# One pipeline for both spatial-gating halves, and block products for all of the output projection

## The chip, the cores and the metric

The kernel runs on one core of a Trainium2 chip. The metric is the time of one execution on the device, in microseconds (us); a kernel's time is the median of several runs. The core has five instruction streams that run side by side and wait for one another through semaphores: TensorE (PE in the profile; PEld are its weight loads), VectorE (DVE), ScalarE (ACT), GpSimd (POOL) and SyncE (SP, which here only issues DMAs). Each stream executes in the order in which it was written.

## The reference

```python
x = A_x                                            # 1 x 2048 x 1024, bfloat16
h = x + _A_ref(_layernorm(x), wq, wk, wv, wo, beta)    # attention with a memory, 32 heads
h2 = h + _B_ref(_layernorm(h), w_in, w_sp, b_sp, w_out)

def _B_ref(x, w_in, w_sp, b_sp, w_out):
    z = _gelu(jnp.einsum('bsd,df->bsf', x, w_in))      # 2048 x 3584
    z1 = z[..., :1792]
    z2 = _layernorm(z[..., 1792:])
    g = jnp.einsum('ts,bsf->btf', w_sp, z2) + b_sp[None, :, None]
    return jnp.einsum('bsf,fd->bsd', z1 * g, w_out)
```

The change lies in the last two lines: the gate g (w_sp is 2048 x 2048), its product with z1, and the output projection with w_out (1792 x 1024), which is added to h.

## The kernel before

Every instruction goes through a recorder (class `_Recorder`, line 34), which keeps one list for each engine in the order of the calls, works out what each instruction depends on, and puts in the waits. So the order of the calls in the text is the order on each engine's queue, and all instructions have line 210 in the profile; one tells them apart by tile names.

The second half of the program, from 412 us on, has these stages.

**z1 (412 to 491 us).** The gating input z1 is computed transposed, in 14 groups of seven products (`z1_step`, line 1199; the order of the steps is that of `offs`). `on(g, k, ...)` hangs other work behind a step: the layer norm of z2, and, later on, the loads, scalings and sums for the first gate. Each group takes PSUM banks from `next_bank()`.

**The gate for output rows 0 to 1023 (`gate(0)`, line 1087; 491 to 575 us).** A block product of 2 x 2 blocks is done with seven products in place of eight. The blocks of w_sp, transposed and scaled to float16, are b11, b12, b22 and b21, and t1 = b12 - b11, t2 = b22 - t1, t3 = b22 - b12, t4 = b21 - t2 are their sums (`sp_sum`, four quarters each). The blocks of z2 have sums too, `s_sum(1..4, g)`, held in the one buffer SS. There are seven column groups g of 128, and each group ("block" in what follows) has seven products of eight matmuls of 512 columns (`prod`):

- p1 (b11) and p2 (b21) add up in bank g % 3. ScalarE copies the bank after p1 (`copy1`), GpSimd adds a bias to that copy twice (`s1b2`, `s1b1`), and after p2 VectorE finishes the bank (`c11`: an eviction and a multiply `out` by z1).
- t2, t3 and t4 add up in bank bb. VectorE reads it after each of them (u2, u3, and an eviction `VB`).
- t1 and b22 add up in bank bc; VectorE reads it after each (`VB`), each time with an `out`.

TensorE's order in a block g is t2, t1, p1(g+2), t3, p2(g+1), t4, b22; for the last groups p1 is left out or moved. VectorE's order is u2, ss4, ss1 and ss2 of the next group, then whatever `each(g, 0)` and `each(g, 1)` hang there, u3, VB, out, ss3, c11, VB, out, VB, out. A product that adds into a bank waits until the bank's reader is done.

**Output for rows 0 to 1023 (`units`, line 1268, and the loop at 1332; 575 to 624 us).** 16 units, each 14 matmuls of 512 columns in bfloat16 (`out_unit`), then one VectorE add and a store. Between the units stand the preparation of the second gate (its 16 transposed loads of w_sp, `sp_half`, `sp_sum`), the loads and squares of w_out (`wo_norm`), and two scale computations (`scale_y`, `scale_w`): ScalarE's squares are summed over partitions by one small product (`total`), reduced by VectorE, raised to a power by GpSimd, and rounded and spread by VectorE (`power`).

**The gate for rows 1024 to 2047 (`gate(1)`, 624 to 708 us).** The same code. `each1` (line 1411) hangs the scaling of w_out's blocks on ScalarE and their sums (`ob_sum`) on VectorE behind its blocks.

**Output for rows 1024 to 2047 (from line 1462; 708 us to the end).** The same seven-product scheme with seven matmuls a product, in four blocks: `o_p1`, `o_p2`, `o_c11`, the sums `y_sum` of the gated rows on VectorE, three adds on GpSimd (`o_adds`). Six matmuls of the first t2 stand between `o_p1(0)` and `o_p2(0)`.

Of the kernel before, what the change touches and what calls it, by code (L numbers as in the profile page):

```python
# [12 lines left out]
T = 2048  # L13
# [3 lines left out]
L = 512  # L17
# [241 lines left out]
def bass_sequential_preLN__memory_aug_infini_attn__mixer_gmlp__prompt_kernel(  # L259
# [31 lines left out]
    class Bump:  # L291
# [4 lines left out]
        def __call__(self, name, shape, dt):  # L296
# [72 lines left out]
    BH = {k: tens(k + "h", [128, 8, L], F16, o * K)  # L369
          for k, o in ROLES + (("t1", 118), ("t2", 190), ("t3", 22), ("t4", 38))}  # L370
# [22 lines left out]
    TW, YS, INVY, SCW, INVO = [b3(k, [128, 1], F32) for k in ("tw", "ys", "invy", "scw", "invo")]  # L393
    SQY = tens("sqy", [128, 28], F32, 768)
    BSQ = tens("bsq", [128, 2], F32, 896)
    TMP = {k: tens("tmp_" + k, [128, L], F32, (4 + 2 * i) * K)
           for i, k in enumerate(("s1", "s1b1", "s1b2", "u2", "u3"))}
    VB = tens("vb", [128, L], BF16, 61 * K)
    SJ = [tens("sj%d" % i, [128, T], BF16, (4 + 4 * i) * K) for i in range(2)]
    BROW = [tens("brow%d" % i, [128, L], BF16, (205 + i) * K) for i in range(2)]  # L400
    WO0 = [tens("w_out0%d" % i, [128, 7, 512], BF16, o * K) for i, o in enumerate((54, 198))]
    WO1 = [tens("w_out1%d" % i, [128, 7, 512], BF16, o * K) for i, o in enumerate((30, 4))]
    WO0H = [tens("w_out0h%d" % i, [128, 7, 512], F16, o * K) for i, o in enumerate((54, 198))]
    FIN2 = tens("fin2", [128, 4, 2, 2, 512], BF16, 14 * K)
    OT4 = [[tens("ot%d%d" % (i, k), [128, 512], F32, (o + 2 * k) * K) for k in range(4)] for i, o in enumerate((38, 118))]
    SY = [tens("sy%d" % i, [128, 4, 7, 128], F16, o * K) for i, o in enumerate((190, 126))]
    FIN = [tens("fin%d" % i, [128, 512], BF16, o * K) for i, o in enumerate((37, 11, 12, 13))]
# [532 lines left out]
    def scale_of(k, n, b):  # L940
        b = next_bank() if b is None else b
        pe.matmul(PS[:, b, 0:n], ONES[:], SQB[:, 0:n], start=True, stop=True)
        dve.tensor_reduce(out=TOT[:], in_=PS[:, b, 0:n], axis=mybir.AxisListType.X, op=ALU.add)
        dve.tensor_single_scalar(TOT[:], TOT[:], 1e-30, ALU.max)
        if k:
            dve.reciprocal(TOP[:], TOT[:])
        else:
            pool.tensor_tensor(TOP[:], TOT[:], MHZ[:], ALU.pow)
# [48 lines left out]
    for r in range(16):  # L997
        q = (37 * r + 15) // 16
        at(q, sp_norm, r)
        if r < 14:  # L1000
            at(q, sp_norm_load, r + 2)
    at(37, pool.tensor_copy, SQB[:, 0:16], SQ[:])
    for k in range(12):
        at(k + 1, wz_norm, (1, 2, 0)[k // 4], k % 4)
# [44 lines left out]
    def sp_load(pr, k, j):  # L1049
        r0, c0 = 1024 * pr + (512 if k in ("b12", "b22") else 0), 1024 if k in ("b21", "b22") else 0  # L1050
        sp.dma_start_transpose(RAW[k][:, :, j * 128:(j + 1) * 128],
                               B_w_sp[r0 + j * 128:r0 + (j + 1) * 128, c0:c0 + 1024])

    def sp_half(k):
        dve.tensor_single_scalar(BH[k][:], RAW[k][:], SC[0][:], ALU.mult)

    def sp_part(k, r):
        s = slice(2 * r, 2 * r + 2)
        act.activation(BH[k][:, s, :], RAW[k][:, s, :], ACTF.Copy, scale=SC[0][:])
# [3 lines left out]
    def sp_sum(o, r=None, eng=dve):  # L1063
        a, b = SUMS[o]
        s = slice(0, 8) if r is None else slice(2 * r, 2 * r + 2)
        eng.tensor_tensor(BH[o][:, s, :], BH[a][:, s, :], BH[b][:, s, :], ALU.subtract)
# [5 lines left out]
    def s_sum(k, g):  # L1072
        if k == 1:
            dve.tensor_tensor(SS[:, 0], a_blk(1, 0, g), a_blk(1, 1, g), ALU.add)
        elif k == 2:
            dve.tensor_tensor(SS[:, 1], SS[:, 0], a_blk(0, 0, g), ALU.subtract)
        elif k == 3:
            dve.tensor_tensor(SS[:, 2], a_blk(0, 0, g), a_blk(1, 0, g), ALU.subtract)
        else:
            dve.tensor_tensor(SS[:, 3], a_blk(0, 1, g), SS[:, 1], ALU.subtract)  # L1080

    def prod(b, a, w, first):
        for i in range(8):
            pe.matmul(bank(b), a[:, i, :], BH[w][:, i, :], start=(first and i == 0), stop=(i == 7),
                      skip_group_check=True)

    def gate(pr, seam=lambda: None, mid=lambda: None, each=lambda g, k: None):
        inv, zo = (INV[0], Z1T) if pr == 0 else (INVY, Z1X)
        t1, t2 = slice(1024 * pr, 1024 * pr + 512), slice(1024 * pr + 512, 1024 * pr + 1024)
        s1, s1b1, s1b2, u2, u3 = (TMP[k][:] for k in ("s1", "s1b1", "s1b2", "u2", "u3"))  # L1090

        def stt(o, b, add):
            dve.scalar_tensor_tensor(o, bank(b), inv[:], add, ALU.mult, ALU.add)

        def out(v, g, i, t):
            dve.tensor_tensor(zo[:, g + 7 * i, t], v, Z1T[:, g + 7 * i, t], ALU.mult)

        def ss(k, g):
            if g < 7:
                s_sum(k, g)  # L1100

        def p1(g):
            prod(g % 3, a_blk(0, 0, g), "b11", True)

        def copy1(g):
            act.activation(s1, bank(g % 3), ACTF.Copy, scale=inv[:])

        def p2(g):
            prod(g % 3, a_blk(0, 1, g), "b21", False)

        def c11(g):
            stt(VB[:], g % 3, BROW[0][:])
            out(VB[:], g, 0, t1)
# [6 lines left out]
        if not pr:  # L1120
            p1(2)
# [3 lines left out]
        for g in range(7):  # L1125
            bb, bc = 3 + g % 2, 5 + g % 2
            prod(bb, SS[:, 1], "t2", True)
            prod(bc, SS[:, 0], "t1", True)
            stt(u2, bb, s1b2)
            if g == 0:  # L1130
                mid()
            ss(4, g)
            if g:
                ss(1, g + 1)
                ss(2, g + 1)
            if 1 - pr <= g <= 3:
                p1(g + 2)
            each(g, 0)
            prod(bb, SS[:, 2], "t3", False)
            if g < 5:  # L1140
                copy1(g + 1)
                p2(g + 1)
            elif g == 5:
                p1(6)
                copy1(6)
            else:
                p2(6)
            each(g, 1)
            stt(u3, bb, s1b2)
            stt(VB[:], bc, u3)  # L1150
            out(VB[:], g, 1, t2)
            if not g:
                ss(1, 1)
                ss(2, 1)
            if g < 6:
                pool.tensor_tensor(s1b2, s1, BROW[1][:], ALU.add)
            ss(3, g + 1)
            if g != 5:
                c11(min(g + 1, 6))
            prod(bb, a_blk(1, 1, g), "t4", False)  # L1160
            each(g, 2)
            stt(VB[:], bb, s1b1)
            out(VB[:], g, 1, t1)
            if g < 6:
                pool.tensor_tensor(s1b1, s1, BROW[0][:], ALU.add)
            prod(bc, SS[:, 3], "b22", False)
            stt(VB[:], bc, u2)
            out(VB[:], g, 0, t2)
            each(g, 3)

    fins = {}

    def fin_load(u, q=sp):
        tc, lo, w = u
        k = len(fins) % 4
        fins[u] = FIN[k]
        q.dma_start(FIN[k][:, 0:w], out2d[tc * 128:(tc + 1) * 128, lo:lo + w])

    def out_unit(u, wsl, q=sp):
        tc, lo, w = u  # L1180
        b = next_bank()
        mm8(PS[:, b, 0:w], lambda i: Z1T[:, i, tc * 128:(tc + 1) * 128], wsl, n=14)
        fin = fins[u]
        dve.tensor_tensor(fin[:, 0:w], fin[:, 0:w], PS[:, b, 0:w], ALU.add)
        q.dma_start(out2d[tc * 128:(tc + 1) * 128, lo:lo + w], fin[:, 0:w])
# [8 lines left out]
    def z1_out(fc, t, src):  # L1194
        act.activation(Z1T[:, fc, t * 512:(t + 1) * 512], src, ACTF.Gelu_apprx_tanh, scale=INV[1][:])
# [54 lines left out]
    for k, g, r in (("b11", 6, 3), ("b12", 6, 3), ("b22", 8, 3), ("b21", 12, 3)):  # L1250
        for j in range(4):
            on(g, r, sp_load, 0, k, j)
    for n, (k, g) in enumerate((("b11", 8), ("b12", 9), ("b22", 11))):
        for r in range(4):
            on(g, (6, 7, 2, 4)[r], sp_part, k, r)
    for r in range(4):
        on(*((10, 6), (10, 5), (11, 6), (11, 5))[r], sp_sum, "t1", r)
        on(*((12, 5), (12, 6), (13, 3), (13, 6))[r], sp_sum, "t3", r)
        on(*((13, 5), (13, 7), (13, 2), (13, 4))[r], sp_sum, "t2", r)
    on(7, 3, brow_load, 0)  # L1260

    offs = {1: -5, 6: 0, 5: 1, 7: 3, 2: 4, 4: 6, 3: 12}
    for x, g, k in sorted((7 * g + offs[k], g, k) for g in range(14) for k in offs):
        z1_step(g, k)
    for i in range(2):
        sp.dma_start(WO0[i][:], wout[:, 7 * i:7 * i + 7, 0:512])

    units = [(tc, 0, 512) for tc in range(6)] + [(tc, 512, 512) for tc in range(8)] + [(tc, 0, 512) for tc in (6, 7)]
    def seam():
        sp_half("b21")  # L1270
        for k in range(1, 4):
            s_sum(k, 0)

    def mid():
        for r in range(4):
            sp_sum("t4", r)

    def z1_norm(g, k):
        for h in range(k and 2):
            r, o = 2 * g + (k > 2), 1024 + 512 * h  # L1280
            if k != 2:
# [252 lines left out]
```

## Time and profile before

| | us |
|---|---|
| median of 3 runs (755.75 to 756.73) | 756.14 |
| span of the profiled execution, first to last instruction | 753.7 |

The page has no time of its own for the profiled execution beside its span; span and median lie 2.44 us apart. By stage, the engines are busy as follows (us, from the table of stretches of time):

| stretch | length | TensorE | VectorE | ScalarE | GpSimd |
|---|---|---|---|---|---|
| z1, 412.06 to 490.76 | 78.7 | 78.7 | 64.0 | 64.6 | 64.3 |
| first gate, 490.76 to 579.00 | 88.2 | 88.2 | 69.9 | 26.3 | 18.9 |
| first output, 579.00 to 623.76 | 44.8 | 44.8 | 25.8 | 17.1 | 1.9 |
| second gate, 623.76 to 708.47 | 84.7 | 84.7 | 69.7 | 18.2 | 18.1 |
| second output, 708.47 to 754.00 | 45.5 | 42.5 | 30.8 | 2.8 | 16.8 |

The granted clock of TensorE is 1.00 in every stretch. In a line of a timeline the columns are the start, the duration, the engine, the operation, the tile written and the tiles read, their shapes and how many instructions were merged; brackets at the end give how long the engine had been idle and who released it. A matmul's duration includes its way through the array (0.38 us), so one reads the pitch from the starts.

### The profile page before, as it was taken

Reading aid. Unit: us, or ns where it says so; the run is one execution under the profiler, and the core shown is the slowest. Engines: PE = TensorE matmul, PEld = TensorE weight load, DVE = VectorE, ACT = ScalarE, POOL = GpSimd, SP = SyncE. Lnnn points to the kernel's source line nnn. Section 1 sums busy time; section 2 is a strip of 40 time slices with the busy share of each in tenths; the row PEclk is TensorE's granted clock in tenths of the full one; section 3 lists DMA queues with packets and bytes.
Section 4 is the critical chain, followed back from the end, with each engine's and each line's share of the span. In section 5 each row is a group of like instructions: output and inputs, shape, how many; then the busy total and the mean of one; then the engine's idle time right before and its main releaser. Section 6 shows DMA issues by size and latency. Waiting matters only on the chain.

```text
span 753.7 us, 13510 instructions
## 1 busy us (share of the span) xinstructions
PE 748.3 (99%) x5470; PEld 359.1 (48%) x5470; DVE 557.1 (74%) x1013; ACT 421.6 (56%) x519; POOL 296.3 (39%) x450
## 2 busy tenths in 40 slices
PE   9999999999999999999999999999999999999998
PEld 4445455555554445545554444444444444444444
DVE  5585589768975576677986796997885385989776
ACT  6777877787777767325894879733231355300000
POOL 2565456555654334010039988622220011222342
PEclk9999999999999999999999999999999999999999
DMA  9554546444523331678650027330019961001211
GB/s 304 171 164 83 96 75 134 99 72 93 120 58 84 119 79 43 162 188 254 192 169 0 1 41 142 56 98 1 0 21 142 262 198 35 0 1 41 79 50 57
DMA packets 136783, 75.09 MB, mean 100 GB/s; under 512 B 98064, under 2 KB 126480, under 8 KB 136720
## 3 DMA queue, kind: packets, MB, share of 16 engines
q1 hardware_dynamic: 129184, 67.14, 37.0%
q10 hardware_dynamic: 7536, 7.08, 3.5%
q8 instruction: 43, 0.70, 0.4%
q14 instruction: 20, 0.16, 0.1%
HBM read 42.74 MB, written 8.39 MB: 68 GB/s over the span
## 4 chain that ended last, share of the span: by engine, by line
PE 90%; DMA 3%; ACT 3%; DVE 2%; POOL 2%; issue 0%; ACTq 0%; DVEq 0%
PE ps L210 90%; DMA sj<-in_B_w_sp_dram 2%; ACT sj L210 2%; POOL zrs L210 1%; DMA wv<-in_A_wv_dram 1%; POOL sz L210 1%; DVE zst L210 1%; ACT z L210 1%; DVE wzh L210 1%; DVE ht L210 0%; DVE zmv L210 0%; ACT L210 0%; DVE fin L210 0%; ACTq L210 0%; DVE top L210 0%
## 5 line engine op out<-in xcount | busy, mean ns | idle before, releaser
L210 ACT ACTIVATE e<-ps 128x2048 bf16<-128x2048 f32 (+1 forms) x96 | 152.6, 1590 | 41.7 <-PE ps L210 41.5
L210 POOL TENSOR_SCALAR_AFFINE_SELECT e<-e 128x512 bf16<-128x512 bf16 x128 | 90.9, 723 | 131.2 <-ACT e L210 131.2
L210 PE MATMUL ps<-win,hnT 128*128 128x448 bf16 x512 | 98.4, 352 | 0.0
L210 POOL TENSOR_TENSOR tmp_s1b<-tmp_s,brow 128x512 f32<-128x512 f32 x28 | 36.4, 1301 | 121.6 <-DVE tmp_u L210 63.0
L210 PEld LDWEIGHTS ps<-win,hnT 128*128 128x128 bf16 x512 | 49.6, 98 | 46.3 <-issue 0.2
L210 PE MATMUL ps<-xnT,wk 128*128 128x512 bf16 x256 | 60.8, 380 | 0.0
L210 DVE TENSOR_TENSOR zt<-ps,zt 128x512 f32<-128x512 f32 x70 | 48.2, 689 | 16.8 <-PE ps L210 13.5
L210 PE MATMUL ps<-xnT,wq 128*128 128x512 bf16 x256 | 60.5, 379 | 0.0
L210 PE MATMUL ps<-wv,xnT 128*128 128x512 bf16 x256 | 60.0, 381 | 0.3 <-DMA wv<-in_A_wv_dram 0.2
L210 PE MATMUL ps<-wo,oT 128*128 128x512 bf16 x256 | 58.0, 379 | 0.0
L210 ACT ACTIVATE z<-ps 128x448 bf16<-128x448 f32 x60 | 30.4, 545 | 33.4 <-PE ps L210 33.4
L210 PE MATMUL ps<-w_out,z1T 128*128 128x512 bf16 x224 | 48.6, 379 | 0.0
L210 DVE BATCH_NORM_STATS2 zst<-z 128x6 f32<-128x448 bf16 x64 | 37.9, 611 | 10.3 <-ACT z L210 10.2
L210 PEld LDWEIGHTS ps<-v,e 128*128 128x128 bf16 x1280 | 38.8, 96 | 14.0 <-issue 6.5
L210 DVE RECIPROCAL rd<-ps 128x16 f32<-128x16 f32 x32 | 8.0, 250 | 47.0 <-PE ps L210 46.8
L210 PE MATMUL ps<-v,e 128*128 128x33 bf16 x1280 | 42.2, 178 | 0.0
L210 ACT ACTIVATE tmp_s<-ps,invy 128x512 f32<-128x512 f32 x7 | 4.8, 688 | 63.3 <-POOL tmp_s1b L210 35.9
L210 POOL TENSOR_TENSOR sz<-wzh 128x512 f16<-128x512 f16 x28 | 34.5, 1232 | 8.3 <-PE ps L210 8.3
L210 PEld LDWEIGHTS ps<-wo,oT 128*128 128x128 bf16 x256 | 24.1, 98 | 27.5
L210 PEld LDWEIGHTS ps<-xnT,wk 128*128 128x128 bf16 x256 | 22.6, 98 | 29.9 <-issue 5.0
L210 ACT ACTIVATE z1T<-zt,inv 128x512 bf16<-128x512 f32 x42 | 29.0, 715 | 13.1 <-DVE zt L210 13.1
L210 PEld LDWEIGHTS ps<-wv,xnT 128*128 128x128 bf16 x256 | 23.1, 98 | 27.3 <-DMA wv<-in_A_wv_dram 0.9
(204 smaller groups left out, 1459.8 us busy)
## 6 DMA issues: line engine op xcount, KB each, us to landing
sj<-in_B_w_sp_dram SPq DMA_DIRECT2D x16, 512.0 KB, 3.7
xch<-in_A_x_dram SPq DMA_DIRECT2D x16, 256.0 KB, 3.7
xr<-in_A_x_dram SPq DMA_DIRECT2D x16, 256.0 KB, 4.0
out_dram<-hch SPq DMA_DIRECT2D x16, 256.0 KB, 2.4
win<-in_B_w_in_dram SPq DMA_DIRECT2D x4, 896.0 KB, 5.3
wz<-in_B_w_in_dram SPq DMA_DIRECT2D x6, 512.0 KB, 8.0
wo<-in_A_wo_dram SPq DMA_DIRECT2D x1, 2048.0 KB, 8.4
fin<-out_dram ACTq DMA_DIRECT2D x16, 128.0 KB, 3.1
```

Source lines behind the costliest of these rows:

```text
L210: ins = getattr(e, op.name)(*op.args, **op.kw)
```

## The change

- `gate` is replaced by `gates_run`, which runs 14 blocks n without a break: n // 7 is the half of the rows, n % 7 the column group. p1(n+2) and p2(n+1) now cross from the first half into the second. In block 6 there is no p2; block 7 has p2(7), c11(7), p1(9) and p2(8). In block 12 p1(13) takes the place of p2. In blocks 6 and 7 the sums ss1, ss2 and ss3 of the next group go to GpSimd.
- The blocks of w_sp for the second half have their own places in SBUF where they can be loaded while the first half runs: b11 and b12 in block 0, b22 in block 5 after its p1, b21 in block 5 after p2. Scaling on ScalarE in blocks 1 to 4 and 6; the 16 quarter sums on VectorE in blocks 6 and 7.
- Both halves of the gated product are kept scaled in float16. So the first half has a scale too, from a bound that is taken from z1's running sums (`accum_out` in `z1_out`, 28 more accumulator reads) and computed in the z1 stage (`bound_z1`, `scale_y(0, ...)`). `scale_y(1, ...)` stands in block 5 between p2 and u3; b_sp is loaded a second time, squared and added to the bound in the stage before z1.
- The blocks of w_out are loaded in blocks 7 and 8 (two loads, and two times seven), squared on ScalarE in blocks 8 to 10 (28 pieces), `scale_w` stands at the end of block 10, scaling in blocks 11 and 12, and the sums in blocks 11 to 13, with t3's two on GpSimd.
- The 16 units of the first output, and their loads and stores on ScalarE's queue, are gone. The output is eight blocks s of the seven-product scheme. The six matmuls of t2 between `o_p1(0)` and `o_p2(0)` are gone, and three first `y_sum` stand in block 13.
- Some tiles move (VB and the biases into the low area, w_out to 22 K and 46 K, and others).

```diff
-    def gate(pr, seam=lambda: None, mid=lambda: None, each=lambda g, k: None):
+    def gates_run(seam, mid, hook):
...
+        for n in range(NG):
+            pr = n // 7
+            bb, bc = 3 + n % 2, 5 + n % 2
+            se = pool if n in (6, 7) else dve
+            prod(pr, bb, SS[:, 1], "t2", True)
+            prod(pr, bc, SS[:, 0], "t1", True)
+            stt(n, u2, bb, s1b2)
+            if n == 0:
                 mid()
+            ss(4, n)
+            if n:
+                ss(1, n + 1, se)
+                ss(2, n + 1, se)
+            if n == 7:
+                p2(7)
+                c11(7)
+            if 1 <= n < 11:
+                p1(n + 2)
+            hook(n, 0)
+            prod(pr, bb, SS[:, 2], "t3", False)
+            if n == 12:
+                p1(13)
+            if n < 13:
+                copy1(n + 1)
+            if n not in (6, 12):
+                p2(min(n + 1, 13))
+            hook(n, 1)
+            stt(n, u3, bb, s1b2)
+            stt(n, VB[:], bc, u3)
+            out(VB[:], n, 1, 1)
...
+            ss(3, n + 1, se)
+            if n not in (6, 12):
+                c11(min(n + 1, 13))
+            prod(pr, bb, a_blk(1, 1, n % 7), "t4", False)
+            hook(n, 2)
+            stt(n, VB[:], bb, s1b1)
+            out(VB[:], n, 1, 0)
...
+            prod(pr, bc, SS[:, 3], "b22", False)
+            stt(n, VB[:], bc, u2)
+            out(VB[:], n, 0, 1)
+            hook(n, 3)
...
     def z1_out(fc, t, src):
-        act.activation(Z1T[:, fc, t * 512:(t + 1) * 512], src, ACTF.Gelu_apprx_tanh, scale=INV[1][:])
+        acc = {"accum_out": SQY[:, 2 * fc + t:2 * fc + t + 1]} if t < 2 else {}
+        act.activation(Z1T[:, fc, t * 512:(t + 1) * 512], src, ACTF.Gelu_apprx_tanh, scale=INV[1][:], **acc)
...
+    def scale_y(pr, n, b):
+        total(n, b)
+        pool.tensor_tensor(TOT[:], TOT[:], TW[:], ALU.mult)
+        power(YS[pr])
+        dve.tensor_tensor(INVY[pr][:], INV[0][:], YS[pr][:], ALU.mult)
...
+    def bound_z1():
+        dve.tensor_reduce(out=TOP[:], in_=SQY[:], axis=mybir.AxisListType.X, op=ALU.max)
+        dve.tensor_single_scalar(TOP[:], TOP[:], 0.341 * 512, ALU.add)
+        dve.tensor_tensor(TOP[:], TOP[:], TOP[:], ALU.mult)
+        dve.tensor_copy(SQB[:, 0:1], TOP[:])
...
+    on(9, 2, bound_z1)
+    on(9, 4, lambda: scale_y(0, 1, next_bank()))
...
+    on(12, 7, brow_scale, 0)
...
+    for j in range(28):
+        do(j // 6, (0, 0, 1, 2, 2, 3)[j % 6], z1_norm, j)
+    do(5, 0, lambda: pool.tensor_copy(SQB[:], SQY[:]))
+    do(5, 1, scale_y, 1, 28, 7)
+    do(5, 3, brow_load, 1, act)
+    do(6, 0, brow_scale, 1)
+    for k, at_ in (("b11", (0, 0)), ("b12", (0, 0)), ("b22", (5, 0)), ("b21", (5, 2))):
         for j in range(4):
+            do(*at_, sp_load, 1, k, j)
+    for r in range(4):
+        do(1 + r // 2, (0, 2)[r % 2], sp_part, 1, "b11", r)
+        do(3 + r // 2, (0, 2)[r % 2], sp_part, 1, "b12", r)
+        do(6, (0, 0, 1, 1)[r], sp_part, 1, "b22", r)
+        do(6, (3, 3, 3, 3)[r], sp_part, 1, "b21", r)
+    for r in range(4):
+        do(6, (0, 0, 1, 1)[r], sp_sum, 1, "t1", r)
+        do(6, 2, sp_sum, 1, "t2", r)
+        do(6 + r // 2, (3, 0)[r // 2], sp_sum, 1, "t3", r)
+        do(7, (0, 0, 1, 1)[r], sp_sum, 1, "t4", r)
...
     def scale_w():
-        total(8)
+        total(28, 7)
         power(SCW)
-        dve.tensor_tensor(INVO[:], YS[:], SCW[:], ALU.mult)
-        dve.reciprocal(INVO[:], INVO[:])
+        for pr in range(2):
+            dve.tensor_tensor(INVO[pr][:], YS[pr][:], SCW[:], ALU.mult)
+            dve.reciprocal(INVO[pr][:], INVO[pr][:])
-
-    for n, u in enumerate(units):
...
+    do(7, 0, ob_load, "b11")
+    do(7, 0, ob_load, "b21")
+    do(7, 3, ob_load, "b12")
+    do(8, 3, ob_load, "b22")
...
+    do(10, 2, lambda: pool.tensor_copy(SQB[:], SQY[:]))
+    do(10, 3, scale_w)
+    for n, (k, h) in enumerate([(k, h) for k in ("b11", "b12", "b22", "b21") for h in range(2)]):
+        do(11 + n // 4, n % 4, ob_scale, k, h)
+    do(11, 3, ob_sum, "t1", 0)
+    do(12, 0, ob_sum, "t1", 1)
+    do(12, 1, ob_sum, "t2", 0)
+    do(12, 2, ob_sum, "t2", 1)
+    do(12, 2, ob_sum, "t3", 0, pool)
+    do(12, 3, ob_sum, "t3", 1, pool)
+    do(13, 0, ob_sum, "t4", 0)
+    do(13, 1, ob_sum, "t4", 1)
+    do(13, 0, fin_in, 0)
+    do(13, 0, fin_in, 1)
+    for x in range(1, 4):
+        do(13, 2, y_sum, x, 0)
+
+    gates_run(seam, mid, hook)
...
     o_p1(0)
-    for x in range(1, 4):
-        y_sum(x, 0, 6, 7)
     o_adds(0)
-    o_prod(3, o_s(2, 0), "t2", True, cs=range(6))
     o_p2(0)
     o_c11(0)
-    for g in range(4):
+    for s in range(8):
...
+        if s < 4:
+            fin_in(s + 4)
```

`hook(n, k)` calls what `do(n, k, ...)` hung at that place, in the order of the `do` calls. The first piece of an `ob_sum` is 2048 columns wide, the second 1536; `y_sum` has the seven chunks of 128 columns of a block at once.

## Prediction

> **What bounds it now.** I read the page's busy shares first, then the end of the chain of waits, then the timeline of single engines in the stages that the change touches, then the groups of instructions by shape.
>
> ```profile
> PE 748.3 (99%) x5470; PEld 359.1 (48%) x5470; DVE 557.1 (74%) x1013; ACT 421.6 (56%) x519; POOL 296.3 (39%) x450
> ```
>
> ```profile
> 412.06 338.53 PE ps L210 x1578
> ```
>
> From 412.06 us to the end TensorE is one unbroken piece of the chain: every product taken away there is gained, every wait put in there is lost, and nothing later gives it back. The pitch of a 512-column product is the distance between starts: eight take 1.727 us in the gates, so 0.2159 us each. What TensorE needs is released by VectorE, and a steady block (12.09 us, seven groups of eight) shows how:
>
> ```profile
> 537.38 1.89 PE L210 MATMUL ps<-t3h,ss 128*128 128x512 f16 x8
> 539.11 1.89 PE L210 MATMUL ps<-b21h,z2h 128*128 128x512 f16 x8
> 540.83 1.89 PE L210 MATMUL ps<-t4h,z2h 128*128 128x512 f16 x8
> ...
> 539.31 0.75 DVE L210 SCALAR_TENSOR_TENSOR tmp_u<-ps,inv,tmp_s1b 128x512 f32<-128x512 f32 x1 [2.04 <-PE ps L210]
> ```
>
> t3 and t4 add into one bank, and between them VectorE must read that bank (u3). It can start 1.93 after t3 starts and takes 0.75 (0.8 until TensorE moves). Before, the b21 group (p2) lies between and covers this. VectorE's own work is some 9.2 us in 12.09. It is longer where GpSimd works too:
>
> ```profile
> 432.21 1.44 POOL L210 TENSOR_TENSOR sz<-wzh 128x512 f16<-128x512 f16 x1 [0.88 <-PE ps L210]
> 433.73 1.49 POOL L210 TENSOR_TENSOR sz<-sz,wzh 128x512 f16<-128x512 f16 x1
> ...
> 432.55 1.64 DVE L210 TENSOR_TENSOR ht<-hnT 128x1024 f16<-128x1024 bf16 x1
> ```
>
> VectorE's sum (0.68 alone) lasts until GpSimd's first has ended at 433.65 and about half a microsecond more; GpSimd's second (1.16 alone) ends later by as much as it was held. So two-input SBUF instructions of the two take turns, whole instruction by whole instruction. Reads of PSUM (0.75) are not held.
>
> **The change part by part.** Times inside a block count from the start of its first group.
>
> 1. *Products saved.* 16 units of 14 (224) become 4 blocks of 49 (196): 28 x 0.2159 = **-6.05**.
>
> 2. *Before the gates.* One more small copy on GpSimd (0.2) stands in its queue where TensorE already waits 1.0 for it at 412: **+0.2** (0 to 0.2). In the gating-input stage the scale for the first half puts eight small VectorE instructions (0.2 each) and two on GpSimd between them; VectorE falls some 1.9 behind at 469, wins back about 0.43 per group in three groups, and then runs without a gap to 497.4, when it releases the first t2 at 497.67. About 0.6 is left, 0.15 of it spare: **+0.5** (0 to 1.0). The 28 accumulator reads (0.19) add 0.75 per group to ScalarE, which idles 1.2 to 1.4 there; without that cover VectorE's sums would be late by the rest.
>
> 3. *Block 5: the second half's scale.* It stands on VectorE ahead of u3, its small product behind p2.
>
> ```profile
> 608.07 0.15 DVE L210 TENSOR_SCALAR tot<-tot 128x1 f32<-128x1 f32 x1
> ...
> 609.51 0.19 POOL L210 TENSOR_TENSOR tot<-tot,tw 128x1 f32<-128x1 f32 x1
> 609.78 0.57 POOL L210 TENSOR_TENSOR top<-tot,mhz 128x1 f32<-128x1 f32 x1
> 610.38 0.15 DVE L210 TENSOR_SCALAR top<-top 128x1 int32<-128x1 int32 x1 [2.16 <-POOL top L210]
> 610.57 0.15 DVE L210 TENSOR_SCALAR ys<-top 128x1 f32<-128x1 f32 x1
> 610.76 0.16 DVE L210 TENSOR_TENSOR invy<-inv,ys 128x1 f32<-128x1 f32 x1
> ```
>
> p2 ends at 8.64; the reduction starts at 8.86, the maximum at 9.06, GpSimd 9.30 to 10.13, three VectorE steps to 10.7, u3 10.70, t4 at 11.5 instead of 8.64: **+2.9** (2.6 to 3.3). Queued behind it are VB, out, ss3 and c11, so VectorE enters block 6 busy until 2.4.
>
> 4. *Blocks 6 and 7: the swap.* Twelve of the sixteen sums for the second half sit in VectorE's order ahead of an u3 or ahead of the t2 and t3 that read them; six s-sums of 1024 columns move to GpSimd. The trace has no such GpSimd sum; its nearest rows bound it:
>
> ```profile
> L210 POOL TENSOR_TENSOR sz<-wzh,sz 128x512 f16<-128x512 f16 x14 | 16.2, 1156 | 0.0
> L210 POOL TENSOR_TENSOR sy<-z1x 128x128 f16<-128x128 f16 x2 | 0.9, 428 | 11.8 <-DVE z1x L210 11.8
> L210 DVE TENSOR_TENSOR t2h<-b22h,t1h 128x1024 f16<-128x1024 f16 x4 | 2.6, 680 | 0.0
> ```
>
> 128 columns 0.43, 512 columns 1.16, so 1.9 ns a column: 1024 take 2.1, 1536 3.1, 2048 4.1. How long one holds VectorE: at least about 1.1 (the longest hold seen), at most its whole length; I take the whole, since every hold seen lasted to the end. Block 6: u2 2.4, ss4 3.1, then from 3.65 four t1 sums (0.6) and GpSimd's two s-sums (2.1) by turns: 10.2. u3 then, t4 at 11.0 instead of 6.91 (p2 no longer covers: 1.0 of this is there in any case): 4.1. Then VB, out and GpSimd's add to 12.45, four t2 sums and ss3 by turns to 16.9; t2 of block 7, due at 14.45, ends at 17.4 instead of 16.2: 1.2. Two evictions, two outs, add, two t3 sums and ss1 to 22.9, u2 to 23.6: t3, due at 22.6, starts 1.05 late. ss4, GpSimd's ss2 (24.2 to 26.3), c11, two t4 sums, the last two t3 sums to 29.0: t3 ends at 29.5 instead of 25.4, 4.1. Together **+10.5**. With no holding at all the same walk gives 1.0 + 0.1 + 0.15 + 1.5 = 2.75; with holds of 1.1, 5.5; with GpSimd at 2.3 a piece and late loads, 12.5.
>
>    The Trainium skill, page "SBUF — State Buffer", section "Who interferes with whom", says that a VectorE instruction with two SBUF inputs and a GpSimd one that reads SBUF exclude each other for the whole instruction, whichever came first; by that these two blocks cost the 10.5, by the longest hold that the rows show, 5.5.
>
> 5. *Block 10 to 11: the scale of w_out.* After out (1.55) the chain of point 3 with four more small steps ends at 3.6, u2 4.4; t3 has no p1 ahead of it here and was due at 3.5: **+0.9** (0.5 to 1.0).
>
> 6. *Blocks 12 and 13: sums of w_out.* Block 12: t1's and t2's pieces (0.87, 1.15) push u3 to 7.3, t4 to 8.1 instead of 7.0: 1.1. Then GpSimd's t3 pieces (4.1, 3.1) hold ss3 and an out: u2 of block 13 only at 17.6 on block 12's clock, t3 at 18.35 instead of 15.05; ss4 behind the second piece, two t4 pieces, u3 23.25, t4 24.05 where an undisturbed pair of blocks has it at 17.27. Together **+6.8**; with no holding 1.2, with holds of 1.1 about 2; up to 7.5.
>
> 7. *Start of the output.* Six t2 products stood between o_p1(0) and o_p2(0) while ScalarE copied the bank (0.69). Now o_p2(0) follows at once: 1.71 + 0.69 + 0.05 - 1.51 = **+0.95** (0.9 to 1.0).
>
> Costed at nothing: the eight output blocks run as four did, TensorE 49 x 0.2159 = 10.6 against VectorE's 6 x 0.75 + 3.8. SP's queue gets the 16 transposes (1.3 each) in blocks 0 and 5, up to 14 us before use; 16 loads of w_out in 7 and 8, read a block later; and eight output loads, each behind the stores of its buffer (1.7) and some 30 us early. ScalarE's norms and scalings fill 7.2 of 12.1 in blocks 1 to 4, 11.2 in block 8. Its bias loads wait for GpSimd's add at 2.15 of block 6, with eight scalings and the copy for block 7 behind them; landing 3.9, b21 is ready at 16.3, needed at 19.1. With the 8.3 us landing that the same load took on this queue, that is gone and 1 to 2 are lost, inside the bound of 12.5.
>
> Sum: -6.05 + 0.2 + 0.5 + 2.9 + 10.5 + 0.9 + 6.8 + 0.95 = **+16.7**. The profiled span 753.7 becomes 770.4; span and median lie 2.44 apart (756.14), so **772.8 us**.
>
> **Rivals.**
> - *B: holds are short.* GpSimd's long sums hold VectorE only for about 1.1 each. For it: no longer hold is shown. Against: none ended early. Points 4 and 6 become 5.5 and 2: +6.9, **763.0**; with no holds, 2.75 and 1.2, +3.3, 759.5.
> - *C, not slower: VectorE keeps up.* In blocks 6, 7, 12 and 13 its own work (24.1 against TensorE's 24.2 in 6 and 7) runs without any hold and every sum is ready when read. Then only the fixed chains are left: 0.2 + 2.9 + 1.0 (u3 of block 6) + 0.9 + 0.95 = 5.95 against 6.05: **756.0**. It decides from the point where all waits stay under 6.05; for a clear gain they must stay under 4.5, so half of block 5's chain must go too. Against it: the sums' place in VectorE's queue, ahead of u3.
> - *D: more is late* than I walked (bias loads, the seam at 497): above 777.
>
> **How the numbers follow.** The forecast has 0.62, B 0.23, C 0.12, D 0.03. The lows of all terms give -6.05 + 0 + 0 + 2.6 + 2.75 + 0.5 + 1.2 + 0.9 = +1.9, 758; the highs +20.5, 777. That range leaves out C, D and a sliver of B, some 0.17. A measurement of this kernel can tell about 0.2% (1.5 us) from no change: C gives 0.05 to faster and 0.07 to the same, all else, 0.88, is slower.
>
> **What would show it.** Right: TensorE idle of 3 us before block 5's t4, 4 before block 6's t4, 4 inside block 7's t3, 3 each before t3 and t4 of block 13, released by VectorE; GpSimd sums of 1024 columns at 2.1 or more; VectorE's t1, t2, t3 sums well over 0.68 on average; 392 output products. Wrong: TensorE unbroken through blocks 6 and 7, GpSimd's 2048-column piece near 2 us, or VectorE's sums at 0.68 beside it.

## The result, and the profile after

| | before | after |
|---|---|---|
| median of 5 runs each, one chip, us | 755.82 (754.87 to 756.73) | 774.49 (769.87 to 775.92) |
| ratio to before, 95% interval | | 1.0241 (1.0214 to 1.0268) |
| span of the profiled execution, us | 753.7 | 768.1 |

The changed kernel is slower by 18.7 us; 772.8 was forecast. The profiled execution of the changed kernel is the shortest of its five (769.87 us).

The page's line of busy time after, and the view of TensorE's waits from 400 us on (total, number and longest, in us), first before, then after:

```profile
PE 747.5 (97%) x5443; PEld 356.5 (46%) x5443; DVE 583.8 (76%) x1041; ACT 449.1 (58%) x607; POOL 334.2 (44%) x468
```

```profile
PE ps L210 <- POOL sz L210: 1.0, 1, 1.0
```

```profile
PE ps L210 <- DVE tmp_u L210: 11.0, 6, 3.4
PE ps L210 <- DVE t3h L210: 2.5, 1, 2.5
PE ps L210 <- DVE zt L210: 1.1, 1, 1.1
PE ps L210 <- ACT ot L210: 0.8, 1, 0.8
PE ps L210 <- POOL sz L210: 0.2, 1, 0.2
```

TensorE has 27 instructions fewer (28 products less, one small total more), and from 400 us on, where it waited once before (1.02 at 412) and was one unbroken piece of the chain from there, it now waits ten times. tmp_u is u2 or u3: the read of a bank by VectorE between two products that add into it. So most of the time is lost because VectorE is late with a read, not because a sum is missing; only t3h is a sum that TensorE waits for itself. The chain of waits (start, length, what) shows in block 6 what VectorE did in that time:

```profile
571.57 0.76 DVE vb L210
572.35 0.43 DVE z1x L210
572.81 0.76 DVE vb L210
573.63 0.36 issue
574.00 0.74 DVE tmp_u L210
574.73 0.60 DVE ss L210
575.33 6.25 DVE t1h L210 x4
581.59 0.67 DVE tmp_u L210
582.31 11.70 PE ps L210 x40
```

Four sums t1h stand in the chain with 6.25 us, and behind them u3 (tmp_u), which ends as TensorE goes on. Such a sum takes 0.68 alone. The timelines of VectorE and GpSimd in the same block, and in block 12, show why it took longer here:

```profile
575.26 6.33 DVE L210 TENSOR_TENSOR t1h<-b12h,b11h 128x1024 f16<-128x1024 f16 x4
...
662.17 4.55 DVE L210 TENSOR_TENSOR ss<-z2h 128x1024 f16<-128x1024 f16 x1
```

```profile
575.51 2.40 POOL L210 TENSOR_TENSOR ss<-z2h 128x1024 f16<-128x1024 f16 x1 [1.73 <-PE ps L210]
577.99 2.45 POOL L210 TENSOR_TENSOR ss<-ss,z2h 128x1024 f16<-128x1024 f16 x1
...
661.92 4.25 POOL L210 TENSOR_TENSOR z2h<-z2h 128x2048 f16<-128x2048 f16 x1
```

Two GpSimd sums lie inside VectorE's four; in block 12 one VectorE sum of 0.68 lasts 4.55, from just behind the start of GpSimd's long one to about half a microsecond behind its end. The hold lasts the whole instruction.

The losses by place, in the profiled execution, are the shifts of the products' starts against the unbroken pitch:

| place | forecast | measured |
|---|---|---|
| products saved | -6.05 | -6.05 (27 instructions fewer = 28 - 1) |
| up to the first gate product | +0.7 | +0.54 |
| block 5, second scale before u3 | +2.9 | +2.80 |
| blocks 6 and 7 | +10.5 | +9.33 |
| block 10 to 11, scale of w_out | +0.9 | +0.72 |
| blocks 12 and 13 | +6.8 | +6.24 |
| start of the output | +0.95 | +0.94 |
| sum against the span | +16.7 | +14.5 (span: +14.4) |

In the four runs that were not profiled the spans are 772.2 to 773.9, at a mean granted clock of 0.989 to 0.991 instead of 0.993; they have no profile, so this table is of the shortest execution alone. The table of stretches (start:end, length, busy time of TensorE, its weight loads, VectorE, ScalarE and GpSimd, then the granted clock, the DMA share and GB/s) has these rows for the end of block 6, for block 7 and for block 13:

```profile
582.31:588.65 6.34, 6.34 (x16) 2.30 (x17) 6.31 (x7) 4.67 (x5) 3.42 (x2) 0.54 0.07 23
588.65:605.33 16.68, 14.16 (x66) 6.08 (x64) 15.24 (x22) 3.46 (x9) 9.68 (x5) 1.00 0.43 112
670.00:676.20 6.20, 4.99 (x16) 1.80 (x16) 6.17 (x7) 0.00 (x0) 2.94 (x1) 0.72 0.11 20
```

After its wait of 3.42 us TensorE ran t4 and most of b22 at half clock, 6.34 us for 16 products that take 3.45 at full clock; after that of 2.92 us in block 13, t3 took 3.10 instead of 1.73. No clock loss was in the forecast.

### The profile page after: what moved, and what is told of

Same layout as the page of the kernel before. It is cut to its first block, busy times and chain, and to the rows that moved or that the text cites. A ratio compares the mean times of both kernels' runs of the same rounds, so it can differ in the third digit from the quotient of the medians.

```text
span 768.1 us, 13613 instructions
## 1 busy us (share of the span) xinstructions
PE 747.5 (97%) x5443; PEld 356.5 (46%) x5443; DVE 583.8 (76%) x1041; ACT 449.1 (58%) x607; POOL 334.2 (44%) x468
## 4 chain that ended last, share of the span: by engine, by line
PE 80%; DVE 9%; DMA 3%; ACT 3%; POOL 2%; issue 1%; SPq 0%; ACTq 0%; DVEq 0%
PE ps L210 80%; ACT sj L210 2%; DMA sj<-in_B_w_sp_dram 2%; DVE vb L210 2%; POOL zrs L210 1%; DVE ss L210 1%; DVE tmp_u L210 1%; DMA wv<-in_A_wv_dram 1%; POOL sz L210 1%; DVE zst L210 1%; DVE t1h L210 1%; DVE z2h L210 1%; DVE z1x L210 1%; ACT z L210 1%; DVE wzh L210 1%
## 5 line engine op out<-in xcount | busy, mean ns | idle before, releaser
L210 POOL TENSOR_TENSOR ot<-ot,fin 128x512 f32<-128x512 f32 x24 | 32.1, 1363 | 51.6 <-ACT ot L210 51.6
L210 ACT ACTIVATE ot<-ps,invo 128x512 f32<-128x512 f32 x8 | 5.5, 688 | 81.7 <-PE ps L210 81.7
L210 PE MATMUL ps<-z2h,sy 128*128 128x512 f16 (+2 forms) x238 | 49.9, 366 | 0.0
L210 ACT ACTIVATE tmp_s<-ps,invy 128x512 f32<-128x512 f32 x14 | 9.6, 683 | 61.7 <-POOL tmp_s1b L210 55.6
```

The lines of the kernel that those rows point to most:

```text
L210: ins = getattr(e, op.name)(*op.args, **op.kw)
```

## The experiments

Each kernel's ratio is to the kernel before, run on the same chip beside it (median there 756.09, 755.72 and 755.42 in the three sets). What an edit wins is the difference of the medians. The profiled executions of the first three single edits have spans of 767.7, 768.4 and 768.4, no shorter than the 768.1 of the changed kernel, whose profiled execution is the shortest of its five; the section on the three edits together compares them place by place.

### The s-sums of blocks 6 and 7 on VectorE

```diff
-            se = pool if n in (6, 7) else dve
+            se = dve
```

> The six s-sums of blocks 6 and 7 stay on VectorE; nothing else differs from the changed kernel (774.5 us). Theory (GpSimd's sums hold VectorE's): VectorE gets 6 x 0.6 = 3.6 us more work, but no sum is held any more. By the same walk, u3 of block 6 starts at 7.5 on the block's clock in place of 9.7, t4 waits 1.3 in place of 3.6, t3 of block 7 still 2.9, and blocks 6 and 7 together take 28.4 in place of 33.5: about 5 us less and less slow clock, 767 to 770 us. Rival (VectorE simply has too much work there, holds don't matter): 3.6 us more work, 2 to 4 us slower, 776 to 779. Second rival (the slow clock after the wait is the main cost): gain only if the wait falls under the one that triggers it, then about 2 to 4 us.

Measured: 769.56 us (766.76 to 770.27), ratio 1.0173 (1.0152 to 1.0193). VectorE has six sums more and is 4.9 us faster with them. Its timeline in block 6:

```profile
578.86 0.69 DVE L210 TENSOR_TENSOR ss<-z2h 128x1024 f16<-128x1024 f16 x1 [0.38 <-PE ps L210]
579.59 0.69 DVE L210 TENSOR_TENSOR ss<-ss,z2h 128x1024 f16<-128x1024 f16 x1
580.20 2.49 DVE L210 TENSOR_TENSOR t1h<-b12h,b11h 128x1024 f16<-128x1024 f16 x4
```

The two s-sums and the four t1 sums take 3.9 us one behind the other; with the first two on GpSimd the four alone took 6.33. TensorE's wait before block 6's t4 falls from 3.42 to 1.13, the one in block 7's t3 from 2.52 to 2.27. No GpSimd sum lies beside VectorE's t1, t2, t3 and t4 sums any more, so what is left there is the sums themselves in this order, not the holds. In this execution half clock followed block 5's wait of 2.63 (t4 took 3.22 instead of 1.73), which it did not in the changed kernel's.

### The second scale one step earlier

The product, the reduction and GpSimd's power go ahead of p2 of block 5 instead of behind it.

```diff
-    do(5, 1, scale_y, 1, 28, 7)
+    do(5, 0, scale_y, 1, 28, 7)
```

> Only the place of the second half's scale in block 5 moves: behind p1(7), before t3, so that VectorE and GpSimd compute it in VectorE's idle time before u3. Theory (the chain in front of u3 costs 2.8, nothing else): TensorE's wait before t4 of block 5 falls from 2.6 to under 0.3, VectorE enters block 6 some 0.6 earlier relative to TensorE: 3 us less, 771 us. Rival (VectorE's lateness only moves into block 6, where the sums decide): within 1 us of 774.5.

Measured: 770.45 us (769.27 to 771.29), ratio 1.0191 (1.0174 to 1.0208). Block 5 has no wait any more. Block 6's t4 still waits 3.18 and block 7's t3 3.90, so the lateness of block 5 was not what made these blocks late.

### The two t3 sums of w_out on VectorE

```diff
-    do(12, 2, ob_sum, "t3", 0, pool)
-    do(12, 3, ob_sum, "t3", 1, pool)
+    do(12, 2, ob_sum, "t3", 0)
+    do(12, 3, ob_sum, "t3", 1)
```

> The two t3 sums of w_out in block 12 stay on VectorE in place of GpSimd (4.25 and 3.27 us there). Theory (held for the whole GpSimd instruction): VectorE's s-sum of 4.55 falls to 0.68 and the one of 2.9 too; it gets 1.2 + 0.95 more work; the wait before t3 of block 13 falls from 3.1 to 1.5, that before t4 from 0.5 to 0, and t3 no longer runs at half clock (1.4): 3.5 to 5 us less, 769 to 771. Rival (VectorE's amount of work decides): 2 us slower, 776.

Measured: 770.7 us (767.94 to 771.8), ratio 1.0189 (1.0167 to 1.0211). In block 13 t3 waits 1.06 instead of 2.92 and runs at full clock, and t4 does not wait.

### Products that keep TensorE busy through the two waits

Sixteen products into a bank that nobody reads stand between block 6's t3 and t4, fourteen ahead of block 13's t3 (`warm_mm`); they are extra work and change no result.

```diff
+            if n == 13:
+                warm_mm(pr, n, 14)
             prod(pr, bb, SS[:, 2], "t3", False)
+            if n == 6:
+                warm_mm(pr, n, 16)
```

> 16 products into an unused bank between t3 and t4 of block 6, and 14 before t3 of block 13, each a little shorter than the wait that stands there; VectorE's order is untouched. Theory on the clock (after a wait of 3 to 5 us TensorE's products run at half clock for some 3 us: t4 and b22 of block 6 took 6.3 in place of 3.45, t3 of block 13 3.1 in place of 1.7): granted clock back to about 0.998, the runs lie closer together, and the time falls by 2 to 6 us (4.3 us of slow products, of which VectorE's lateness in block 7 takes part back): 769 to 772. Rival (VectorE's lateness sets the end, the slow products are hidden under it): within 1 us of 774.5.

Measured: 774.01 us (773.12 to 775.58), ratio 1.0241 (1.0224 to 1.0257): no change. TensorE in blocks 6 and 7 of this kernel:

```profile
582.52 1.90 PE L210 MATMUL ps<-t4h,z2h 128*128 128x512 f16 x8
584.25 1.89 PE L210 MATMUL ps<-b22h,ss 128*128 128x512 f16 x8
586.56 2.41 PE L210 MATMUL ps<-t2h,ss 128*128 128x512 f16 x8 [0.42 <-DVE t2h L210]
...
599.82 1.89 PE L210 MATMUL ps<-t3h,ss 128*128 128x512 f16 x4 [4.21 <-DVE t3h L210]
601.50 3.62 PE L210 MATMUL ps<-b21h,z2h 128*128 128x512 f16 x8
```

The clock stayed up where block 6's wait had been, t4 and b22 take 1.73 each, and TensorE arrives at block 7's t2 and t3 that much earlier, to wait there: 0.42 before t2, 0.42 before t3 and 4.21 within it, instead of nothing and 2.52. Then the rest of t3 and p2 run at half clock (3.41 for p2's eight products). So this kernel does not take the slow clock away; it comes a block later.

The kernel of the edit before has no extra product there, and its t4 ran at full clock all the same:

```profile
583.61 1.90 PE L210 MATMUL ps<-t4h,z2h 128*128 128x512 f16 x8 [3.43 <-DVE tmp_u L210]
```

Its waits in block 7 are the same (0.42, 0.43 and 4.20). Blocks 6 and 7 lost 12.2 us in it and 12.4 with the extra products, against 9.33 in the changed kernel's profiled execution, where t4 and b22 were slow. One reason stands in VectorE's t3 sums of block 6, in the changed kernel and in the kernel of the edit before:

```profile
590.44 1.28 DVE L210 TENSOR_TENSOR t3h<-b22h,b12h 128x1024 f16<-128x1024 f16 x2
```

```profile
591.75 3.21 DVE L210 TENSOR_TENSOR t3h<-b22h,b12h 128x1024 f16<-128x1024 f16 x2
```

They start 8.13 and 8.14 us behind block 6's t4. GpSimd's next s-sum waits for TensorE: behind the slow products it starts at 10.04, too late to meet them, at full clock at 8.27, and holds them. So a full clock for t4 alone wins nothing, as VectorE and the holds set the time of block 7; what a full clock behind every wait would be worth, these runs do not show.

### The three edits together

> The three single edits together: the s-sums of blocks 6 and 7 on VectorE, the second scale one step earlier, the t3 sums of w_out on VectorE. Theory (each takes a loss of its own place): the gains add, 774.5 - (774.5 - 769.6) - (774.5 - 770.45) - (774.5 - 770.7) = 774.5 - 4.9 - 4.05 - 3.8 = 761.7, within 760.5 to 763. Rival (blocks 5 to 7 are one piece of lateness, as VectorE has more work there than TensorE has products, so the first two gains are in part the same microseconds): 764 to 767, with a wait of TensorE of 3 us or more left in block 6 or 7.

The edit is the first three diffs. Measured: 760.92 us (759.03 to 762.1), ratio 1.006 (1.0041 to 1.0078), where the sum of the three single gains gives 761.7. The waits that are left in blocks 5 to 7 are 1.13, 0.24 and 2.48. The losses add; the rival of one common lateness fell.

That each is lost in its own place shows in the profiled executions, by the starts of three products (us):

| kernel | first gate product to block 8's t2 | block 8's t2 to the output's first product |
|---|---|---|
| changed kernel | 114.03 | 74.35 |
| s-sums on VectorE | 111.91 | 74.36 |
| second scale one step earlier | 112.85 | 74.34 |
| t3 sums of w_out on VectorE | 116.90 | 70.45 |
| extra products | 117.08 | 74.35 |
| the three edits together | 108.26 | 70.44 |

The third edit changes nothing ahead of block 12, so its 116.90 is a second execution of the changed kernel's code in the first stretch, 2.87 us longer than the profiled one. Against it the first edit wins 5.0 us, the second 4.05 and both 8.6, much as the medians say (4.9 and 4.05); against the changed kernel's own profile they win 2.1 and 1.2. In the second stretch the third edit wins 3.9 in both kernels that have it, and block 13's slow t3 cost nothing: 74.35 with it in the changed kernel, 74.34 to 74.36 where t3 ran at full clock.

### The second half's sums moved into VectorE's idle time

In the changed kernel none of the 16 sums for the second half is made before block 6: t1 goes to the place of the first half's t1, which block 6's product still reads, t2 and t3 need b22, which is scaled in block 6, and t4 needs t2. Here t1 is written over b12, and t3 is formed as t2 - b11. That is the same sum with two roundings to float16 more, and it lets t1 be made two blocks earlier.

```diff
-                                       ROLES1 + (("t1", 118), ("t2", 190), ("t3", 198), ("t4", 38))))]
+                                       ROLES1 + (("t1", 198), ("t2", 190), ("t3", 118), ("t4", 38))))]
...
-        a, b = SUMS[o]
+        a, b = ("t2", "b11") if pr and o == "t3" else SUMS[o]
...
-                p2(7)
-                c11(7)
+                sp_sum(1, "t4", 0)
+                sp_sum(1, "t4", 1)
...
-            if n not in (6, 12):
+            if n != 12:
                 p2(min(n + 1, 13))
...
-        do(6, (0, 0, 1, 1)[r], sp_part, 1, "b22", r)
-        do(6, (3, 3, 3, 3)[r], sp_part, 1, "b21", r)
+        do(5, 1, sp_part, 1, "b22", r)
+        do(6, 0, sp_part, 1, "b21", r)
...
-        do(6, (0, 0, 1, 1)[r], sp_sum, 1, "t1", r)
-        do(6, 2, sp_sum, 1, "t2", r)
+        do(4 + r // 3, 0, sp_sum, 1, "t1", r)
+        do(6, 0 if r < 3 else 2, sp_sum, 1, "t2", r)
```

Besides, the first two edits above are in, b21 is loaded one step earlier, the bias loads are on SP and their scaling stands a step later, b12 and b22 are scaled earlier, copy1(7) and ss1 and ss2 of block 8 change place, and p1(10) goes to the front of block 8.

> w_sp's second half is prepared earlier and with VectorE's slack instead of against it: t1 = b12 - b11 is written over b12 in blocks 4 and 5, t3 is formed as t2 - b11, b22 is scaled in block 5, b21 loaded right behind p2(6), so that p2(7) stands in block 6 again; 4 sums fall in block 6, 8 in block 7; the s-sums are on VectorE, the second scale one step earlier; the end of the stage is as in the changed kernel. Theory (what blocks 5 to 7 lost, 2.80 + 9.33 = 12.1 us, was VectorE's work against its slack of about 2.7 us a block, made worse by the holds): 774.5 - 12.1 + (0 to 2 for block 7, which still has 2.4 us too much) = 762.4 to 764.4, and no wait of TensorE over 1 us between block 5 and block 9. Rival (only holds and the scale cost; the sums are hidden): no better than those two edits add, 774.5 - 4.9 - 4.05 = 765.6 or more.

Measured: 759.83 us (759.3 to 760.46), ratio 1.0054 (1.004 to 1.0068), 2.6 lower than the theory's lower end. The theory took from the changed kernel's median the 12.1 us that its shortest execution lost in blocks 5 to 7; the kernel of the third edit, with the same code there, lost 2.8 + 12.2 = 15.0, which gives 759.5. The one wait between block 5 and block 9, on TensorE, and VectorE's order in block 7:

```profile
579.54 0.60 PE L210 MATMUL ps<-b21h,z2h 128*128 128x512 f16 x2 [0.43 <-ACT b21h L210]
```

```profile
586.03 2.49 DVE L210 TENSOR_TENSOR t3h<-t2h,b11h 128x1024 f16<-128x1024 f16 x4
588.44 0.69 DVE L210 TENSOR_TENSOR ss<-z2h,ss 128x1024 f16<-128x1024 f16 x1
589.04 1.29 DVE L210 TENSOR_TENSOR t4h<-b21h,t2h 128x1024 f16<-128x1024 f16 x2
590.54 0.75 DVE L210 SCALAR_TENSOR_TENSOR tmp_u<-ps,invy,tmp_s1b 128x512 f32<-128x512 f32 x1 [0.22 <-PE ps L210]
```

Seven sums stand ahead of block 7's u3, and VectorE still idles 0.22 before it. The same work in another order hides; what the changed kernel lost here is order and holds, not too little of VectorE. How the gain divides among the edits that this kernel makes at once is not shown.

### All the losses taken away

As the last kernel, and: z1's scale in two steps (`scale_z`: the total and GpSimd's part; `scale_z2`: VectorE's three small steps), so that VectorE makes evictions while GpSimd works; w_out's norms all by block 9, its scale ahead of block 10's t3, its scaling from block 10 on, its sums on VectorE in blocks 11 to 13; and t2's product between o_p1(0) and o_p2(0).

```diff
-    on(9, 4, lambda: scale_y(0, 1, next_bank()))
+    on(9, 4, scale_z)
+    on(10, 5, scale_z2)
...
-    do(10, 3, scale_w)
+    do(10, 0, scale_w)
...
     o_p1(0)
     o_adds(0)
+    o_prod(3, o_s(2, 0), "t2", True)
     o_p2(0)
```

> As the run before, and: z1's scale split so that VectorE doesn't wait for GpSimd's power (its wait was 1.07 us), the norm of w_out one block earlier with its scale ahead of block 10's t3, w_out's sums all on VectorE at two a block (11 to 13), t2's product of the first output step ahead of p2 there (0.94 us). Theory (all the losses but block 7's rest and the wait after attention go; the six products saved stay): 774.5 - 20.6 + (0 to 3) = 754 to 757, just about the kernel before or 1 to 2 us under it. Rival (work that is moved collides in the new place, above all ScalarE's 14 norms in block 9 and VectorE's sums in block 13): 757 to 761.

Measured: 753.23 us (752.34 to 753.87), ratio 0.9966 (0.9954 to 0.9979): this one is faster than the kernel before, by 0.3%, and 0.8 under the range that was expected. Besides the wait at 412, TensorE's waits in the profile are 0.42 (b21 in block 6), 0.96 (u3 of block 12) and 0.91 (the first output sum).

### Two sums of w_out later

```diff
-    do(12, 0, ob_sum, "t2", 1)
+    do(12, 2, ob_sum, "t2", 1)
...
-    do(13, 3, ob_sum, "t4", 1)
...
         o_stt(s, f12[:], bb, f12[:])
+        if s == 0:
+            ob_sum("t4", 1)
```

> From the run with all edits (753.2), whose profile has TensorE wait 0.96 us for u3 in block 12, behind two t2 sums of w_out, and 0.91 us for the first sum of the output stage, behind a t4 sum: the second t2 sum goes behind block 12's t4, the second t4 sum behind that first output sum. Theory (VectorE's order is all that is late): 753.2 - 1.9 = 751.3, within 750.7 to 752. Rival (VectorE has too much work from block 11 on, and the wait moves to block 13's u3 or to t4 of the output's first step): 752.3 to 753.5, with a new wait of 0.5 us or more there.

Measured: 751.2 us (750.16 to 753.18), ratio 0.9949 (0.9935 to 0.9962), 4.2 us under the kernel before. All that the view of TensorE's waits has left from 400 us on:

```profile
PE ps L210 <- ACT b21h L210: 0.4, 1, 0.4
PE ps L210 <- POOL sz L210: 0.2, 1, 0.2
```

From the product that waits behind the attention (412.06 before, 411.07 here) to the last one (749.28 and 744.04) it is 337.2 before and 333.0 here: 4.25 of the 6.05 us that the 28 products are worth, 0.43 given to b21, the rest to gaps of up to 0.4 that the view does not list (block 11's t3 starts 2.00 after t1, not 1.73).

### GpSimd sums where VectorE has slack

From the kernel of 753.2 us; the six s-sums that blocks 2 and 3 make go to GpSimd.

```diff
-            se = dve
+            se = pool if n in (2, 3) else dve
```

> From the run with all edits (753.2): the s-sums for blocks 3 and 4 are given to GpSimd in blocks 2 and 3, where VectorE has no other sums to make (its idle time there is 2.04 + 0.37 + 0.38 us a block). Theory (a GpSimd sum of about 2.4 us costs time only by what of it holds VectorE beyond its idle time): six holds of which VectorE meets about 1.5 us a block, all covered: 753.2 within 0.6, no wait of TensorE in blocks 2 to 5, and VectorE operations with two inputs from SBUF stretched to 1 us and over. Rival (a sum on GpSimd costs its own extra 1.7 us each wherever it stands, so that the price in blocks 6 and 7 was slowness and not lack of slack): six such sums, 5 us or more over 753.2.

Measured: 753.43 us (753.25 to 754.65), ratio 0.9973 (0.9962 to 0.9985): no loss. GpSimd and VectorE in block 2:

```profile
524.27 2.12 POOL L210 TENSOR_TENSOR ss<-z2h 128x1024 f16<-128x1024 f16 x1 [2.42 <-PE ps L210]
526.47 2.12 POOL L210 TENSOR_TENSOR ss<-ss,z2h 128x1024 f16<-128x1024 f16 x1
...
529.66 2.30 POOL L210 TENSOR_TENSOR ss<-z2h 128x1024 f16<-128x1024 f16 x1
```

```profile
527.68 0.75 DVE L210 SCALAR_TENSOR_TENSOR tmp_u<-ps,invy,tmp_s1b 128x512 f32<-128x512 f32 x1 [3.83 <-PE ps L210]
...
530.02 0.75 DVE L210 SCALAR_TENSOR_TENSOR vb<-ps,invy,brow 128x512 bf16<-128x512 f32 x1
530.81 1.44 DVE L210 TENSOR_TENSOR z1x<-vb,z1T 128x512 f16<-128x512 bf16 x1
```

While VectorE idles (3.83), two of GpSimd's sums pass; the second lies beside the start of u3 too, which reads PSUM and keeps its 0.75. The third, from 529.66 to 531.96, lies beside two VectorE instructions: the eviction, which reads PSUM and one SBUF row, keeps its 0.75; the multiply of two SBUF inputs, 0.42 alone, lasts until 532.25. So the slow GpSimd sum has no price of its own here. What counts is whether a two-input SBUF instruction that stands ahead of a bank's read meets it, and whether idle time covers the hold.

## Why the prediction was right

**The mechanism** held in the gates and the output: the 28 products saved are worth 6.05 us by the pitch, and 4.25 of it is seen as won in the last kernels; reads of banks by VectorE come late in blocks 5, 6, 7, 11, 12 and 13, and in 6, 7, 12 and 13 GpSimd's long sums make them later. What it lacked is the half clock behind the waits; what it had in the wrong place is point 2.

- *Point 2, ahead of the gates.* The place was wrong. The forecast let VectorE's lateness run on to the seam at 497 (+0.5), where TensorE does not wait. It is lost at once, before the product at 469.61 (a wait of 1.07; 1.24 by the starts):

```profile
466.75 0.15 DVE L210 TENSOR_SCALAR tot<-tot 128x1 f32<-128x1 f32 x1
467.85 0.15 DVE L210 TENSOR_SCALAR top<-top 128x1 int32<-128x1 int32 x1 [0.95 <-POOL top L210]
468.04 0.15 DVE L210 TENSOR_SCALAR ys<-top 128x1 f32<-128x1 f32 x1
468.23 0.72 DVE L210 TENSOR_TENSOR invy<-inv,ys 128x1 f32<-128x1 f32 x1
468.88 0.68 DVE L210 TENSOR_TENSOR zt<-ps,zt 128x512 f32<-128x512 f32 x1
```

  VectorE sits idle 0.95 inside the chain, and the read of a bank (zt) that TensorE needs stands behind it. Nor is a cost of the small copy seen at 412: that wait is 0.16 in the profile of after and 0.16 to 1.54 in the other kernels, which have the same copy, so it varies by itself. That the stage's sum, +0.54, is near the +0.7 of the forecast is luck: the short wait at 412 won 0.86 of the 1.24 back.
- *Point 3*, 2.9: 2.80, and gone when the chain goes ahead of p2. Mechanism and size right.
- *Point 4*, 10.5: 9.33 in the profile. In the kernel of the third edit, with the same code, it is 12.2, so the forecast lies between two executions. Of its parts, the 4.1 before block 6's t4 is 3.58; GpSimd's sums take 2.40 and 2.45 there, not 2.1, but VectorE came in a little earlier. The 1.2 in t2 of block 7 is nothing and the 5.15 in t3 is 2.86, because TensorE itself came 2.89 later, on the half clock after its wait: a term that the forecast did not have lay over two that it had. The kernels of the third edit and of the extra products show that it is so: with t4 at full clock, waits of 0.42 before t2, 0.42 before t3 and 4.2 within it come back. The value between the two bounds was chosen rightly: by the longest hold that was seen before (1.1) the two blocks would have cost 5.5.
- *Point 5*, 0.9: 0.72.
- *Point 6*, 6.8: 6.24, of it 1.37 by the half clock, which hides most of the second wait in block 13 (0.67 instead of 2.4; in the kernel of 759.8, where t3 ran at full clock there, it is 1.88). GpSimd's pieces took 4.25 and 3.27, forecast 4.1 and 3.1.
- *Point 7*, 0.95: 0.94.
- *Costed at nothing.* The output's eight blocks run without a wait, the bias loads were ready in time, and ScalarE's norms disturbed nothing. That was right.

**Rival B** (short holds, 763.0) fell by the 4.55 us hold, and by the 4.9 and 3.8 us that two edits win, each of which only moves sums from GpSimd to VectorE. **Rival C** (VectorE keeps up, 756.0) is false for the change as written, and its opposite, that VectorE has too little time for the sums, fell as well: the kernels with another order have the same sums and almost no wait. **Rival D** (more is late, above 777) did not come: the seam at 497 and the bias loads cost nothing.

**The total** is nearer than its terms, and that is in part luck. The terms sum to 14.5 in the profiled execution, 2.2 less than forecast, and its span is 768.1, not 770.4. The forecast then added 2.44 to come from the span to the median; here the median lies 6.4 above that span: 1.8 between the span and the time of the same execution, and 4.6 because this one is the shortest of five. Where the others lost their time is not shown, since one execution of each kernel is profiled. Two things point to it. The third edit's kernel, with the same code up to block 11, loses 2.87 more in blocks 6 and 7, and its first gate product starts at 492.60 instead of 491.30. And the granted clock of the other four runs is lower by 0.002 to 0.004, which is worth 1.5 to 3.1 us (an estimate: 768 us by the difference); but the kernel with extra products has 0.993 to 0.996 and the same time, so the clock alone does not explain them.

## What to carry to other kernels

When two products add into one bank and a third engine reads between them, ask what stands in front of that read in the reader's queue; sums that are needed a block later belong behind it, and a block's idle time (here 2.8 us of 12.1) is the budget. Give work to GpSimd where VectorE idles or only reads PSUM; beside VectorE's two-input SBUF sums it holds them for its full length. Before a change that saves products is dropped because it lost time, move its side work about: here the same 28 products are worth -4.2 us or +18.7 us.

## What the runs showed of the hardware

- A wait of TensorE can be followed by half clock: 0.54 was granted in the 6.34 us behind a wait of 3.42 us. No sharp threshold shows. Waits of 4.21, 4.20, 3.90, 3.42 and 3.18 were followed by it, one of 3.43 was not; 2.92 in one kernel was, 2.92 and 2.93 in others were not; 2.63 in one was and in another was not, as block 5's t4 shows in the kernel with the s-sums on VectorE (3.43) and in the changed kernel (1.90):

```profile
570.05 3.43 PE L210 MATMUL ps<-t4h,z2h 128*128 128x512 f16 x8 [2.63 <-DVE tmp_u L210]
```

```profile
568.35 1.90 PE L210 MATMUL ps<-t4h,z2h 128*128 128x512 f16 x8 [2.63 <-DVE tmp_u L210]
```

  The shortest that was followed by slow products is 2.27, in block 7 of the kernel with the s-sums on VectorE (p2 took 2.96 instead of 1.73). The Trainium skill, page "TensorE: Matmul & The Clock Gate", section "What's actually happening", has the clock at half rate after at least one idle window of about 3.4 us. Here shorter waits were enough in some executions, and the one of 3.43 was not.
- A VectorE instruction with two SBUF inputs that meets a GpSimd sum lasts to its end or a little longer (4.55 beside 4.25, 1.44 beside 2.30), and one that reads PSUM and one SBUF input does not (0.75 beside 2.30). This agrees with the Trainium skill, page "SBUF — State Buffer", section "Who interferes with whom", by which a VectorE instruction with at most one SBUF input, outside the two-port modes, does not contend with GpSimd.
- A float16 sum of 1024 columns on GpSimd takes 2.12 us when VectorE leaves it alone, and 0.68 on VectorE.
